# Seven block products in place of eight for the first expert layer of the last batch, with partial sums chained in PSUM

## The chip, the cores and the metric

The kernel runs on one core of one Trainium2 chip. The metric is the device time of one execution in microseconds (us). Before the change it was 373.66 us, the median of 3 runs (373.06 to 373.91). The profile comes from one execution of the kernel; its span, from the first to the last instruction, is about 1.8 us shorter than the device time of the same execution.

## The reference

Block-sorted attention is followed by a mixture of four experts. Only the second part is changed.

```python
def _moe_ref(x, domain_probs, w1, w2):
    N, D, E, F = (3072, 512, 4, 1024)     # from the setup
    p = domain_probs / (domain_probs.sum(-1, keepdims=True) + 1e-09)
    out = np.zeros((N, D), dtype=np.float32)
    for e in range(E):
        h = np.maximum(x @ w1[e], 0.0)          # first layer
        out += p[:, e:e + 1] * (h @ w2[e])      # second layer
    return out
```

`x` is the attention's output: 4 batches of 768 tokens. The kernel takes a batch's tokens in three chunks of 256. While it computes the experts of one batch, it interleaves the attention of the next one, so only the last batch has nothing beside it.

## The kernel before

The first layer (line L735 in the profile) multiplies 128x128 blocks of weights with 256 tokens at a time, 32 matmuls per expert and chunk. VectorE evicts the result: relu, times the expert's probability, into `Hb`. The second layer (L769) is already in seven block products. Its inputs are `Hb` and sums of its blocks (`Sb`), which VectorE makes in `h_sums`.

```python
def h_sums(e, which):                       # all on VectorE, two SBUF inputs each
    if which == 1:   tt(sm[0], blk(0, 1), blk(1, 1), ALU.add)
    elif which == 2: tt(sm[1], sm[0], blk(0, 0), ALU.subtract)
    elif which == 3: tt(sm[2], blk(0, 0), blk(0, 1), ALU.subtract)
    else:            tt(sm[3], blk(1, 0), sm[1], ALU.subtract)

def chunk_first(b, c, es, first, slot):
    for e in es:
        for g in range(2):
            ps = psm([P, 4, 2 * P], F32, ...)
            for f in range(4):
                for kc in range(NKC):                        # L735
                    nc.tensor.matmul(ps[:, f, :], w1sb[e][:, kc, ds((4 * g + f) * P, P)],
                                     xT[:, kc, ds(2 * c * P, 2 * P)],
                                     start=(kc == 0), stop=(kc == NKC - 1))
            nc.vector.scalar_tensor_tensor(out=Hb[:, e, ds(4 * g, 4), :], in0=ps[:], scalar=0.0,
                                           op0=ALU.max, in1=<probability>, op1=ALU.mult)
            if e > first:
                for w in ((1,), (2, 3))[g]:
                    h_sums(e - 1, w)                         # between the experts
            slot()                                           # work of the next batch's attention
```

The natural-order keys, values and queries of a batch come into tiles of a rotating pool, the queries into a single one:

```python
nat = ctx.enter_context(tc.tile_pool(name="nat", bufs=2))
...
natural[(b, "q")] = nat.tile([P, NPB, R, 2, D], F16, name=f"natq_{b}", tag="natq", bufs=1)
```

The loads of batch 1 are emitted early in the program, ahead of the first expert layer of batch 0 (`load_natural(1, ...)`, `load_queries(1, ...)`).

The softmax here doesn't subtract the row's maximum and nothing guards it: scores larger than these inputs give would overflow.

## Time and profile before

| | before |
|---|---|
| device time, median | 373.66 us |
| span of the profiled run | 371.0 us |
| TensorE busy | 362.8 us (98%) |
| last batch, chunk | 13.97 us first layer + 12.23 us second layer |
| the wait of TensorE for the queries of batch 1 | 1.8 us |

The prediction shows the page's first line, the chain of the last batch and the two stretches of its last chunk. Two more views matter here. The first is the page's list of groups: line, engine, operation, output and input, shapes, count; then the busy time and the mean nanoseconds of one; then the idle time of the engine before them, and what ended it.

```profile
L735 PE MATMUL ps_h<-xT,w 128*128 128x256 f16 x1440 | 163.3, 273 | 0.0
L741 DVE SCALAR_TENSOR_TENSOR Hb<-ps_h,pb 128x1024 f16<-128x1024 f32 x90 | 110.1, 1223 | 40.3 <-PE ps_h L735 38.7
```

The mean of 273 ns in the first line is the time of one matmul from issue to end. Matmuls overlap, so the cost of one in a row is the busy time over the count: 163.3/1440 = 0.113 us over the whole kernel, and 0.109 us in the last batch. VectorE's eviction of 1024 elements has 40.3 us of idle time ahead of it, nearly all of it waiting for TensorE: VectorE has time left.

The second view is the chain of work that ended last, where batch 1 starts (start, length, what):

```profile
68.92 6.63 DMA natq<-in_q_dram
...
75.56 7.31 DMA qT<-natq
```

Here transfers carry the chain for 14 us on end: the queries are loaded for 6.63 us, then transposed by a second transfer for 7.31 us, and TensorE waits for that at 82.9 us.

### The profile page before, as it was taken

The page shows a single profiled execution, that of the slowest core. Times are in us where ns is not written, and L with a number is a line of the kernel's source. Part 1 is how long each engine was busy: PE and PEld are TensorE (multiplying, and loading weights), DVE is VectorE, ACT ScalarE, POOL GpSimd, SP SyncE. Part 2 cuts the span into 40 slices and gives each one's busy share as a digit, 9 for nine tenths or more (in the row PEclk, how much of TensorE's full clock was granted, in tenths as well). Part 3 has the DMA queues.
Part 4 walks back from the last instruction along what each step waited for, and adds up shares of the span by engine and source line. Part 5 has one row for each costly group of instructions (what it writes and reads, how often), then busy time and mean ns, then how long its engine had stood idle before and what let it go on. Part 6 is the DMA issues. An engine that isn't in the chain of part 4 may idle for free.

```text
span 371.0 us, 9075 instructions
## 1 busy us (share of the span) xinstructions
PE 362.8 (98%) x3939; PEld 314.8 (85%) x3939; DVE 259.9 (70%) x469; ACT 87.8 (24%) x157; POOL 86.0 (23%) x122
## 2 busy tenths in 40 slices
PE   8899999989999999999999999999999999999996
PEld 8785858869888888998898888998888888888885
DVE  5654798666988784696695684696695693774873
ACT  2664330534230334222100335222101000000000
POOL 8872101803486303001911000000000001001001
PEclk9999999999999999999999999999999999999999
DMA  8999999998999868741972322604204101121001
GB/s 118 208 206 230 208 209 197 187 163 107 178 160 164 110 87 125 139 81 43 123 69 52 101 63 63 142 3 79 80 0 80 59 12 46 58 44 55 18 0 58
DMA packets 69748, 38.25 MB, mean 103 GB/s; under 512 B 40391, under 2 KB 64717, under 8 KB 69709
## 3 DMA queue, kind: packets, MB, share of 16 engines
q0 software_dynamic: 34640, 17.83, 39.1%
q1 hardware_dynamic: 35068, 19.85, 27.2%
q8 instruction: 31, 0.51, 0.5%
q14 instruction: 9, 0.07, 0.1%
HBM read 42.00 MB, written 6.34 MB: 130 GB/s over the span
## 4 chain that ended last, share of the span: by engine, by line
PE 85%; DMA 7%; DVE 4%; ACT 2%; POOL 1%; issue 1%; DVEq 0%; ACTq 0%
PE ps_h L735 39%; PE ps_p L769 33%; PE ps_h L640 3%; DMA xT<-xsl 3%; PE ps_o L675 3%; DMA qT<-natq 2%; DMA natq<-in_q_dram 2%; PE ps_s L398 1%; PE ps_a L430 1%; PE ps_k L379 1%; PE ps_v L346 1%; PE ps_mk L467 1%; DVE xsl L415 1%; PE ps_s L522 1%; DMA sn<-in_sort_net_dram 0%
## 5 line engine op out<-in xcount | busy, mean ns | idle before, releaser
L735 PE MATMUL ps_h<-xT,w 128*128 128x256 f16 x1440 | 163.3, 273 | 0.0
L735 PEld LDWEIGHTS <-w 128*128 128x128 f16 x1440 | 139.6, 98 | 17.3
L741 DVE SCALAR_TENSOR_TENSOR Hb<-ps_h,pb 128x1024 f16<-128x1024 f32 x90 | 110.1, 1223 | 40.3 <-PE ps_h L735 38.7
L769 PEld LDWEIGHTS <-Sb 128*128 128x128 f16 x720 | 69.8, 98 | 9.0 <-issue 0.3
L769 PEld LDWEIGHTS <-Hb 128*128 128x128 f16 x540 | 52.2, 98 | 6.1
L800 POOL TENSOR_TENSOR oa<-u,p 128x256 f32<-128x256 f32 x9 | 6.5, 721 | 175.7 <-issue 160.9
L769 PE MATMUL ps_p<-w,Sb 128*128 128x256 f16 x360 | 43.3, 273 | 0.1
L769 PE MATMUL ps_p<-w,Hb 128*128 128x256 f16 x360 | 43.1, 273 | 0.0
L769 PE MATMUL ps_p<-T,Sb 128*128 128x256 f16 x360 | 42.1, 273 | 0.0
L388 ACT CAST kT<-ps_k 64x384 f16<-64x384 f32 x48 | 22.7, 473 | 37.9 <-PE ps_k L379 37.0
L405 ACT ACTIVATE ET<-ps_s 96x768 f16<-96x768 f32 x24 | 18.0, 802 | 46.5 <-PE ps_s L398 46.5
L784 ACT COPY p<-ps_p 128x256 f32<-128x256 f32 x9 | 3.3, 372 | 90.5 <-PE ps_p L769 68.1
L114 POOL DMA_DIRECT2D natq<-in_q_dram x24 | 19.8, 851 | 13.3 <-DMA w<-in_moe_w_dram 9.3
L769 PE MATMUL ps_p<-T,Hb 128*128 128x256 f16 x180 | 21.6, 273 | 0.0
L720 DVE TENSOR_TENSOR Sb<-Sb,Hb 128x512 f16<-128x512 f16 x45 | 18.8, 418 | 0.4
L722 DVE TENSOR_TENSOR Sb<-Hb 128x512 f16<-128x512 f16 x45 | 18.8, 418 | 0.0
L718 DVE TENSOR_TENSOR Sb<-Hb 128x512 f16<-128x512 f16 x45 | 18.7, 416 | 0.0
L415 DVE TENSOR_TENSOR xsl<-ps_a,rz 96x512 f16<-96x512 f32 x24 | 16.5, 687 | 1.1 <-DMA xT<-xsl 0.3
L724 DVE TENSOR_TENSOR Sb<-Hb,Sb 128x512 f16<-128x512 f16 x45 | 16.6, 427 | 0.0
L798 DVE TENSOR_TENSOR u<-ps_p,p 128x256 f32<-128x256 f32 x9 | 3.8, 425 | 17.4 <-PE ps_p L769 17.4
L352 ACT CAST vo<-ps_v 128x768 f16<-128x768 f32 x12 | 9.5, 801 | 20.0 <-PE ps_v L346 19.3
L103 POOL DMA_DIRECT2D nat_k<-in_k_dram x8 | 6.1, 760 | 32.0 <-PE ps_k L379 27.1
(132 smaller groups left out, 298.3 us busy)
## 6 DMA issues: line engine op xcount, KB each, us to landing
w<-in_moe_w_dram POOLq DMA_DIRECT2D x7, 1024.0 KB, 26.5
pb<-p_dram SPq DMA_DIRECT2D x12, 512.0 KB, 5.1
nat_k<-in_k_dram POOLq DMA_DIRECT2D x8, 384.0 KB, 8.1
nat_v<-in_v_dram POOLq DMA_DIRECT2D x8, 384.0 KB, 8.7
vs<-vo SPq DMA_DIRECT2D x36, 66.0 KB, 4.5
natq<-in_q_dram POOLq DMA_DIRECT2D x24, 96.0 KB, 6.3
out_dram<-ob SPq DMA_DIRECT2D x9, 256.0 KB, 2.1
out_dram<-oa SPq DMA_DIRECT2D x8, 256.0 KB, 2.3
```

Of the source, the lines that this page charges most:

```text
L114: nc.gpsimd.dma_start(t[:, h // 2, :, h % 2, :], q[b, h].rearrange("(t p) d -> p t d", p=P))
L388: nc.scalar.copy(kT[ds(D * hh, D), r], pk[ds(D * r, D), hh].rearrange("p a (i c) -> p a i c", c=CP),)
L405: nc.scalar.activation(ETs[2 * (pr % 2) + hh][:, 0:S].rearrange("c (a x) -> c a x", a=2), pss[hh][0:BLK, :, 0:HS], AF.Exp, bias=0.0, scale ...
L415: nc.vector.tensor_tensor(xsl[:, :, hh, :].rearrange("c (a i) d -> c a i d", a=2), av[:, :, :, 0:D], rz[:].broadcast_to([BLK, 2, HB, D]), ...
L640: nc.tensor.matmul(ps[:, f % 2 if nq == 2 else f // 2, ds(0 if nq == 2 else (f % 2) * n, n)], w1sb[0][:, kc, ds((m * g + f) * P, P)], xT[: ...
L718: tt(sm[0], blk(0, 1), blk(1, 1), ALU.add)
L720: tt(sm[1], sm[0], blk(0, 0), ALU.subtract)
L722: tt(sm[2], blk(0, 0), blk(0, 1), ALU.subtract)
L724: tt(sm[3], blk(1, 0), sm[1], ALU.subtract)
L735: nc.tensor.matmul(ps[:, f, :], w1sb[e][:, kc, ds((4 * g + f) * P, P)], xT[:, kc, ds(2 * c * P, 2 * P)], start=(kc == 0), stop=(kc == NKC ...
L741: nc.vector.scalar_tensor_tensor(out=Hb[:, e, ds(4 * g, 4), :], in0=ps[:], scalar=0.0, op0=ALU.max, in1=pb[:, ds(e, 1), :].broadcast_to([P ...
L769: nc.tensor.matmul(ps[:], lhs(e, f), Ts[e][rhs][:, f, :], start=(e == es[0] and f == 0), stop=(e == E - 1 and f == KH - 1),)
```

## The change

The intent is to save an eighth of TensorE's multiplications in the first layer of the last batch: seven block products in place of eight, as the second layer does already. Each product is 8 matmuls of 128 columns. The partial sums that several products share are not added by VectorE: ScalarE copies product 1 from one PSUM bank into another, and the next products accumulate on top of it. The weight sums need space, which the attention's dead buffers give in the last batch; for that these buffers become slices of one large tile, the arena.

```diff
+    arena = const.tile([P, 4 * NW + NQ + 4 * 4 * P + R * 4 * VW], F16, name="arena")
 ...                                    # keys, values, queries, masks and vo become slices of it:
-            natural[(b, "q")] = nat.tile([P, NPB, R, 2, D], F16, name=f"natq_{b}", tag="natq", bufs=1)
+            natural[(b, "q")] = arena[:, ds(4 * NW, NQ)].rearrange("p (n t h d) -> p n t h d", n=NPB, t=R, h=2)
 ...                                    # attention tiles on 128 partitions in place of 96:
-            vs = att.tile([BLK, NB, 4, VW], F16, name=f"vs_{b}_{qd}", tag="vs")
+            vs = att.tile([P, NB, 4, VW], F16, name=f"vs_{b}_{qd}", tag="vs")[0:BLK]
 ...                                    # the loads of batch 1 are emitted later
+    def input_sums(e, n):              # 16 weight sums, in batch 2
+        nc.vector.tensor_tensor(a[dst], a[x], a[y], op)
+    def token_sums(c):                 # 4 sums of token blocks per chunk
+        ...
+    def last_banks(n):                 # re-divides the PSUM: banks X, Z, Q
+        ...
+        nc.tensor.matmul(last["X"][n][:], w1sb[0][:, 0, 0:P], w1sb[0][:, 1, 0:512], start=True, stop=True)
+    def seven(c, e):
+        def product(dst, lhs, rhs, first=False):
+            for f in range(KH):
+                for k in range(2):
+                    nc.tensor.matmul(
+                        dst[:, ds(f * P, P)], a[lhs][:, k, ds(f * P, P)], t[rhs][:, k, :],
+                        start=(first and f == 0 and k == 0), stop=(f == KH - 1 and k == 1), ...)
+        def p1(): product(Z, "a11", "b11", True);  nc.scalar.copy(X, Z)
+        def p5(): product(Q, "s1", "t1", True)
+        def p6(): product(X, "s2", "t2");          nc.scalar.copy(u2, X)
+        def p2(): product(Z, "a12", "b21");        finish(0, 0, Z)            # VectorE
+        def p7(): product(X, "s3", "t3");          nc.scalar.copy(u3, X); tt(t22, Q, u3, ALU.add)
+        def p4(): product(X, "a22", "t4");         finish(1, 0, X)            # VectorE
+        def p3(): product(Q, "s4", "b22");         tt(t12, Q, u2, ALU.add)
+        # blocks 22 and 12: relu on ScalarE, then the multiplication on GpSimd
+    def last_chunk(c):
+        ...                            # products of the four experts, then the second layer:
+        for e in range(E - 1):
+            h_sums(e, 1)
+        tt(oa1, product("p2", blk(1, 0), "b21"), p1[:], ALU.add)
+        ...
```

## The prediction

> **What bounds the kernel now.** I read the page's busy shares first, then its chain of work that ended last, then the busy time by stretch for the last batch, which is the only part whose arithmetic changes.
>
> ```profile
> PE 362.8 (98%) x3939; PEld 314.8 (85%) x3939; DVE 259.9 (70%) x469; ACT 87.8 (24%) x157; POOL 86.0 (23%) x122
> ...
> PE 85%; DMA 7%; DVE 4%; ACT 2%; POOL 1%; issue 1%; DVEq 0%; ACTq 0%
> ```
>
> ```profile
> 289.01 13.97 PE ps_h L735 x128
> 302.99 12.23 PE ps_p L769 x112
> ...
> 341.41 13.97 PE ps_h L735 x128
> 355.38 12.24 PE ps_p L769 x112
> ```
>
> The first fence is of the page, the second is the chain in order of time (start, length, what). TensorE is 98% busy and carries 85% of the chain; and from 289.01 on to 367.62 us the chain is TensorE alone: three chunks, each 128 matmuls of the first layer in 13.97 us and 112 of the second in 12.23 us, with no wait between them. The 3.4 us after 367.62 are the last sum and store and stay as they are. So one matmul of 256 columns costs 13.97/128 = 0.1091 us there, and what TensorE saves in a first layer is saved in full, unless a wait appears.
>
> ```profile
> core 0: us, PE busy (x) PEld busy (x) DVE busy (x) ACT busy (x) POOL busy (x), PEclk, DMA share, GB/s
> ...
> 341.40:355.40 14.00, 14.00 (x131) 12.55 (x129) 11.15 (x15) 0.00 (x0) 0.00 (x0) 1.00 0.10 39
> 355.40:367.60 12.20, 12.20 (x112) 10.69 (x110) 6.60 (x14) 1.12 (x3) 1.45 (x2) 1.00 0.04 12
> ```
>
> VectorE is busy 11.15 of 14.0 us in a first layer, ScalarE and GpSimd do nothing there. The change will use those two.
>
> The price of the new matmul (128 columns, each with a weight load of its own) is in the timeline: 30 of them in a row early on, and six in batch 1.
>
> ```profile
> 9.05 1.85 PE L241 MATMUL ps_w<-Hb 128*128 128x128 f16 x30
> ...
> 100.53 0.51 PE L379 MATMUL ps_k<-PIk,nat_k 128*128 128x128 f16 x6 [0.23 <-DVE xsl L415]
> 100.62 0.69 DVE L415 TENSOR_TENSOR xsl<-ps_a,rz 96x512 f16<-96x512 f32 x1
> 100.82 0.70 PEld L735 LDWEIGHTS <-w 128*128 128x128 f16 x7
> 100.87 0.82 PE L735 MATMUL ps_h<-xT,w 128*128 128x256 f16 x6
> ```
>
> One such matmul lasts 0.219 us by itself (that line's median). Thirty: (1.85-0.219)/29 = 0.0562 us each. Six different weights: (100.87-100.53)/6 = 0.057. I take 0.056.
>
> **What the Trainium skill says.** "TensorE: Matmul & The Clock Gate", section Back-to-back issue gap, gives N/2.4 + 2.5 ns for an isolated stream, 55.8 ns at 128 columns, but also a sustained 81 ns per pair of weight load and matmul at 128 columns. The trace agrees with the first (0.056) and not with the second, in short bursts only. "PSUM — Partial Sum Buffer", The four PSUM rules: a matmul without the first flag accumulates where an earlier matmul has set the bit, and ScalarE's writes leave these bits alone. That is what lets ScalarE copy product 1 into a second bank and the next products add on top; no run of before shows it. "SBUF — State Buffer", SBUF: two separate sides: a VectorE operation with two SBUF inputs and a GpSimd operation exclude each other for the whole instruction. The trace agrees:
>
> ```profile
> 366.46 0.72 POOL L803 TENSOR_TENSOR ob<-u,p 128x256 f32<-128x256 f32 x1 [1.03 <-DVE u L801]
> 366.48 0.99 DVE L804 TENSOR_TENSOR ob<-ob,u 128x256 f32<-128x256 f32 x1
> ```
>
> VectorE's sum takes 0.99 us beside GpSimd's, where the same size with one input in PSUM takes 0.425.
>
> **The change, part by part.**
>
> *TensorE, first layer.* Per chunk and expert, 32 matmuls of 256 columns become 7 products of 8 matmuls of 128 columns. Per chunk: 4 x 56 x 0.056 = 12.54 us in place of 13.97, so 1.43 saved; three chunks: 4.3 us. The columns fall by an eighth (8192 to 7168 per expert: 32 x 256 against 56 x 128), which alone would be 13.97/8 = 1.75; the fixed part of a matmul, paid 224 times in place of 128, takes the rest.
>
> *Added on TensorE:* two throw-away matmuls of 512 columns when the PSUM pools are re-divided, 0.2 us each: +0.4.
>
> *Weight sums.* Sixteen VectorE sums of 128x1024 f16, 0.69 us each as L706 has them, 11 us in all, plus four token sums of 128x256 (some 0.3 each, estimated) per chunk. They stand in batch 2. There VectorE waits in most second layers (busy 8.4 to 9 of 13 us), and the dead buffers' last readers are done well before by the order of instructions. The crowded place is the last chunk of batch 2: in 276.0 to 289.0 it is busy 8.4 us of 13.0, and gets nine of the sums (6 us) and four token sums. Walking its queue: oa's first half ended at 282.55 and gets three sums ahead of it, near 284; three more behind it, and the p6 sum ends near 287 in place of 286.0; one more, and the first token sum ends about 288.0, while TensorE, after p7 (287.1 plus 0.2), reaches the product that needs it at about 287.75. I put +0.3 for batch 2.
>
> *The pace of one expert.* Seven products of 0.446 us are 3.12 us. Sizes for 512 columns: ScalarE copies 256 in 0.372 (L784) and 384 in 0.473 (L388), so 512 in about 0.58; VectorE 0.69 (L415 has 0.687, half of L741's 1.22 plus the fixed part agrees); GpSimd has 0.72 for 256 in f32 (L803) and 1.04 for 512 in f16 (L319), so about 1.25 for 512 in f32 (estimate). Per expert ScalarE has five (2.9 us), VectorE four (2.8), GpSimd two (2.5): all three fit into 3.12, by little. A reader starts 0.24 us after TensorE has left a product (p1 of a second layer starts at 302.82, 16 x 0.109 later is 304.57, and its copy starts at 304.81). The tightest wait: product 1 ends at 0.45, its copy runs 0.69 to 1.27, product 2 may write that bank again at 1.31 and is due at 1.34, behind products 7 and 5. The second: product 7 ends 0.89, its copy ends 1.8, the VectorE sum 2.5, product 3 is due at 2.67. So it just fits. I charge 0.05 per expert for misfits: 12 x 0.05 = +0.6.
>
> *The turn into the second layer.* All Hb sums, formerly between the experts, now come after the last expert, and two of the four Hb blocks come from GpSimd. Times from the start of the last expert's product 7, TensorE without waits: p2 of the second layer ends at 4.84, p4 at 6.58, and p5 then needs the bank of p2, freed by VectorE's p2 sum; p5's last quarter, at 7.89, needs the last expert's first Hb sum. GpSimd still has four multiplications of 1.25: 0.5 to 1.8, 1.9 to 3.1, 3.1 to 4.4, and the last not before 4.7, because its input (product 3 at 3.1, VectorE to 4.0, ScalarE to 4.6) is late. VectorE reaches its Hb sums, two SBUF inputs each, at 4.0 and must wait for GpSimd. If it gets in at 4.4, three sums of 0.34 and the p2 sum end at 5.9, in time; GpSimd's last then runs 5.5 to 6.75, the next three sums wait for it and end at 7.8, and the last expert's first sum at 8.2 makes p5 wait 0.3. If GpSimd keeps the port through its fourth, to 6.0, the p2 sum ends at 7.4 and p5 waits 0.85. I take 0.5 per chunk, +1.5.
>
> Sum: -4.3 + 0.4 + 0.3 + 0.6 + 1.5 = -1.5 us, rounded to 372.0 from 373.66.
>
> Batches 0 to 2 keep their order on every engine apart from the sums; loads of batch 1 are emitted later but stand at the same place of the queue. I give them 0.
>
> **The rivals.**
> 1. *Nothing waits.* The queues fit as counted and GpSimd is quicker than I think: -4.3 + 0.4 + 0 to 0.3 = 369.9. For it: every wait in the expert loop has a slack of 0 or more, so the order was fitted to these durations. Against: slack of 0.03 us.
> 2. *An engine takes over.* If a ScalarE copy from PSUM into PSUM, which before nowhere has, is 0.1 longer, product 2 waits each time and the five copies reach 3.4 us, so the pace is ScalarE's: 12 x 0.3 = 3.6 us back, near 374.5 with the turn's wait.
> 3. *The short matmuls run at the skill's sustained 81 ns.* 672 x 0.081 = 54.4 against 41.9 us: +12.5, near 386. Against it, besides the 0.056: L430's 16 matmuls of 65 columns with a weight load each take 0.48 us, 0.030 each, so a load does not cost 0.08.
> 4. *The lock at the turn is worse*, 1.2 us per chunk: 374.
>
> **Range and chances.** 369.6 is rival 1 with a little luck, 374.4 is rivals 2 or 4; I hold 8 in 10 between. Faster by 2% would need 7.5 us, more than TensorE saves in all: 1%. Slower by 2% needs rival 3 or a mistake of mine: 3%.
>
> **What would show it.** Right: first layers of the last batch near 12.6 to 12.9 us with 224 matmuls at 0.056; a wait of TensorE of about half a microsecond at the second layer's p5, released by VectorE, with GpSimd busy until then; second layers near 12.7 net of the next chunk's products. Wrong: a pace of one expert well over 3.2 us with ScalarE without idle time (rival 2); matmul pitch of 0.08 (rival 3); no wait at p5 (rival 1); or a loss in batch 2 over 1 us, at the weight sums.

## The result, and the profile after

The changed kernel ran in 369.52 us, median of 4 runs (369.09 to 370.15), beside 373.79 us of the kernel before on the same chip (373.06 to 374.86). A ratio in this document is the mean time of one kernel's runs over that of the other's runs of the same rounds, so it is not quite the ratio of the medians quoted. Here it is 0.9885, with a 95% interval of 0.9857 to 0.9913. The prediction had 372.0 and the range 369.6 to 374.4, so the result lies just below the range.

The page's first line and the chain by engine:

```profile
PE 358.5 (97%) x4229; PEld 313.8 (85%) x4229; DVE 277.5 (75%) x521; ACT 121.5 (33%) x217; POOL 118.6 (32%) x146
...
PE 80%; DMA 11%; DVE 5%; POOL 1%; issue 1%; ACT 1%; DVEq 0%; ACTq 0%
```

TensorE has 4.3 us less work in more instructions, ScalarE and GpSimd have 38% more each, and VectorE 18 us more. The chain is still TensorE's.

The chain in the last batch, one expert of the new first layer (start, length, what):

```profile
293.60 0.45 PE ps_Q L981 x8
294.04 0.45 PE ps_Z L981 x8
294.49 0.45 PE ps_X L981 x8
294.94 0.45 PE ps_Q L981 x8
295.38 0.45 PE ps_Z L981 x8
295.83 0.89 PE ps_X L981 x16
296.72 0.45 PE ps_Q L981 x8
```

Seven products of 8 matmuls follow on each other without a gap, and the same point of the next expert comes at 296.72: 3.12 us per expert, 56 matmuls, 0.0557 us each. No other engine appears. The groups that run beside them:

```profile
L994 POOL TENSOR_TENSOR Hb<-tmp,pb 128x512 f16<-128x512 f32 x24 | 30.9, 1293 | 20.2 <-ACT tmp L993 19.0 <-DVE Sb L725 0.6
L993 ACT ACTIVATE tmp<-tmp 128x512 f32<-128x512 f32 x24 | 15.2, 635 | 3.2 <-DVE tmp L1025 2.6 <-DVE tmp L1017 0.6
L1016 ACT COPY tmp<-ps_X 128x512 f32<-128x512 f32 x12 | 7.1, 591 | 0.6 <-PE ps_X L981 0.6
L1001 ACT COPY ps_X<-ps_Z 128x512 f32<-128x512 f32 x12 | 6.8, 570 | 15.9 <-PE ps_Z L981 15.9
```

The copy from PSUM into PSUM takes 0.570 us, the copies out of it 0.586 (L1008) and 0.591, and each of the two relus 0.635. The five durations of ScalarE add up to 0.570 + 0.586 + 0.591 + 2 x 0.635 = 3.02 of the 3.12 us, but this sum is not what ScalarE needs. The timeline of one expert, with the TensorE product (p2) that must wait for the first copy:

```profile
294.57 0.57 ACT L1001 COPY ps_X<-ps_Z 128x512 f32<-128x512 f32 x1 [0.21 <-PE ps_Z L981]
295.05 0.59 ACT L1016 COPY tmp<-ps_X 128x512 f32<-128x512 f32 x1
295.22 0.61 PE L981 MATMUL ps_Z<-xT,w 128*128 128x128 f16 x8
296.37 0.59 ACT L1008 COPY tmp<-ps_X 128x512 f32<-128x512 f32 x1 [0.20 <-PE ps_X L981]
```

Operations that follow directly on each other overlap: the second copy starts 0.48 us after the first, which lasts 0.57. ScalarE is idle for 0.21 and 0.20 us in an expert in the middle of the loop, waiting for TensorE, so it has about 0.4 us to spare. p2 starts 0.08 us after the copy that it waits for has ended.

At the turn into the second layer the chain leaves TensorE, once in each chunk. The timeline of that stretch, without the rows that matter less (start, length, engine, line, operation, count, idle time before it and what ended it), and under it what the trace says of the three sums in it (shortest, median and longest in ns):

```profile
302.10 2.51 POOL L994 TENSOR_TENSOR Hb<-tmp,pb 128x512 f16<-128x512 f32 x2
...
304.14 2.49 DVE L725 TENSOR_TENSOR Sb<-Hb 128x512 f16<-128x512 f16 x3
...
304.97 1.38 POOL L994 TENSOR_TENSOR Hb<-tmp,pb 128x512 f16<-128x512 f32 x1 [0.36 <-ACT tmp L993]
305.01 1.91 PE L1069 MATMUL ps_Q<-T,Hb 128*128 128x256 f16 x16
...
306.56 0.41 DVE L1090 TENSOR_TENSOR oa<-ps_Q,p 128x256 f32<-128x256 f32 x1
...
307.02 1.95 PE L1069 MATMUL ps_Q<-w,Sb 128*128 128x256 f16 x16
```

```profile
L725 DVE TENSOR_TENSOR Sb<-Hb x3: 412/747/1487, 304.1 to 305.1; 128x512 f16<-128x512 f16 x3
```

TensorE issues p4 from 305.01 on; 16 matmuls at 0.109 us end at 306.76, and p5 starts only at 307.02. It needs the bank that VectorE's sum at 306.56 reads. That sum had its input since about 305.2, but VectorE was still in the third of its three `Hb` sums, which began at 305.14 and took 1.487 us in place of 0.412: GpSimd's multiplication ran from 304.97 to 306.35. The chunks follow at 25.09 us (p5 at 307.02, 332.11 and 357.20) where they took 26.20 before.

The stretch where batch 1 starts, in the chain:

```profile
69.16 5.88 DMA arena<-in_q_dram
...
75.06 7.09 DMA qT<-arena
```

Both transfers are a little shorter than before (5.88 for 6.63, 7.09 for 7.31), and TensorE waits 0.8 us for them, not 1.8.

To split the gain I cut the chain of each kernel where the second layer of batch 2's last chunk begins, and where the last product ends:

| | up to the cut | from the cut to TensorE's end | then |
|---|---|---|---|
| before | 276.30 | 91.32 | 3.4 |
| after | 275.93 | 88.47 | 3.3 |
| difference | -0.4 | -2.85 | -0.1 |

The second column is firm: two more runs of the changed kernel give 88.47 too, and a second one of the kernel before 91.33. The first column varies by 0.4 to 0.7 us between profiles of one kernel, so it needs several. Over all kept profiles whose clock was not lowered before the cut, it is 276.30 and 276.91 us with the old buffers (before, before_again) and 274.72 to 276.33, mean 275.69, in thirteen with the new place of the query buffer: some 0.9 us less. The second column shows that the last batch alone gave 2.85 us, where the prediction had 1.5.

### The profile page after: what moved, and what is told of

Its sections match the earlier page's. It is cut to its first block, busy times and chain, and to the rows that moved or that the text cites. A ratio compares the mean times of both kernels' runs of the same rounds, so it can differ in the third digit from the quotient of the medians.

```text
span 367.7 us, 9859 instructions
## 1 busy us (share of the span) xinstructions
PE 358.5 (97%) x4229; PEld 313.8 (85%) x4229; DVE 277.5 (75%) x521; ACT 121.5 (33%) x217; POOL 118.6 (32%) x146
## 4 chain that ended last, share of the span: by engine, by line
PE 80%; DMA 11%; DVE 5%; POOL 1%; issue 1%; ACT 1%; DVEq 0%; ACTq 0%
PE ps_h L742 28%; PE ps_p L777 23%; PE ps_Q L1069 8%; PE ps_X L981 4%; DMA w<-in_moe_w_dram 4%; DMA xT<-xsl 3%; PE ps_Q L981 3%; PE ps_Z L981 3%; PE ps_o L682 3%; DMA qT<-arena 2%; DMA arena<-in_q_dram 2%; PE ps_h L647 1%; PE ps_s L405 1%; DVE Sb L725 1%; PE ps_a L437 1%
## 5 line engine op out<-in xcount | busy, mean ns | idle before, releaser
L742 PE MATMUL ps_h<-xT,w 128*128 128x256 f16 x1056 | 121.0, 273 | 0.0
L742 PEld LDWEIGHTS <-w 128*128 128x128 f16 x1056 | 102.1, 98 | 13.1
L748 DVE SCALAR_TENSOR_TENSOR Hb<-ps_h,pb 128x1024 f16<-128x1024 f32 x66 | 80.7, 1223 | 29.5 <-PE ps_h L742 29.0
L777 PEld LDWEIGHTS <-Hb 128*128 128x128 f16 x396 | 38.1, 98 | 4.6
L994 POOL TENSOR_TENSOR Hb<-tmp,pb 128x512 f16<-128x512 f32 x24 | 30.9, 1293 | 20.2 <-ACT tmp L993 19.0
L777 PE MATMUL ps_p<-w,Hb 128*128 128x256 f16 x264 | 31.6, 273 | 0.0
L777 PE MATMUL ps_p<-w,Sb 128*128 128x256 f16 x248 | 29.9, 273 | 0.1
L120 POOL DMA_DIRECT2D arena<-in_q_dram x24 | 19.9, 853 | 12.1 <-DMA w<-in_moe_w_dram 9.7
L981 PEld LDWEIGHTS <-w 128*128 128x128 f16 x384 | 23.3, 98 | 0.4
L981 PEld LDWEIGHTS <-arena 128*128 128x128 f16 x288 | 17.4, 98 | 0.1
L993 ACT ACTIVATE tmp<-tmp 128x512 f32<-128x512 f32 x24 | 15.2, 635 | 3.2 <-DVE tmp L1025 2.6
```

The lines of the kernel that those rows point to most:

```text
L120: nc.gpsimd.dma_start(t[:, h // 2, :, h % 2, :], q[b, h].rearrange("(t p) d -> p t d", p=P))
L777: nc.tensor.matmul(ps[:], lhs(e, f), Ts[e][rhs][:, f, :], start=(e == es[0] and f == 0), stop=(e == E - 1 and f == KH - 1),)
L981: nc.tensor.matmul(dst[:, ds(f * P, P)], a[lhs][:, k, ds(f * P, P)], t[rhs][:, k, :], start=(first and f == 0 and k == 0), stop=(f == KH - ...
L994: nc.gpsimd.tensor_tensor(Hb[:, e, ds(i * KH, KH), ds(j * P, P)], src.rearrange("p (f x) -> p f x", f=KH), pb[:, ds(e, 1), ds(j * P, P)].b ...
```

## The experiments

Sixteen runs followed. My theory after the result had four parts: the first layer is 1.47 us faster per chunk and nothing else waits in it; the turn costs about 0.3 us per chunk, through VectorE's order behind GpSimd; the weight sums cost nothing; and the new buffer layout gives about 1 us at the start of batch 1. The rivals were that these shares are chance, that the later emission of the loads is what helps, and that ScalarE is near the bound.

### after_again: the changed kernel unedited, five rounds

> The changed kernel once more, unedited, in five rounds, to learn how large the gain is: the two profiles differ by 3.3 us of span, the medians of four runs by 4.3. Theory A (the gain lies in the last batch alone): 3.1 us, from counting TensorE between the start of the second layer of batch 2's last chunk and the end (91.48 before, 88.40 after). Theory B (about 1 us more is gained in batches 0 to 2, where I had put 0): 4.0 to 4.5 us.

Measured: 369.8 us (median) beside 373.96, ratio 0.989 (0.9864 to 0.9917). The gain of 4 us stands.

### layout_only: arena, wider tiles and later loads, but the old last batch

```diff
-        if b == B - 1:                    # of the changed kernel
-            for c in range(R // 2):
-                last_chunk(c)
-            break
-                if b == B - 2: ...        # weight sums, prepare_last, token_sums, last_begin
```

> The changed kernel with its one arena, the later emission of batch 1's loads and the wider tiles, but with the old last batch, no weight sums, no re-divided PSUM. Theory A: 0 against the kernel before, within 0.3 us. Theory B: 0.7 to 1.3 us faster than the kernel before. In the profile the last batch must run at 13.97 and 12.23 us per layer as before.

Measured: 372.81 us beside 373.96, ratio 0.9976 (0.9949 to 1.0002). The interval touches 1, but the trace agrees with a gain: TensorE waits 1.3 us for the queries and is busy 54.64 us from 62 to 118 us, where the kernel before has 1.8 and 53.85.

### layout_and_sums: the same, with the sixteen weight sums in batch 2

```diff
+                if b == B - 2:
+                    for cc, n, e, m in PLAN_A:
+                        if (cc, n) == (c, at[0]):
+                            input_sums(e, m)
```

The result of the sums isn't used; the one that would overwrite a weight writes a dead block instead.

> As layout_only, with the sixteen VectorE weight sums of 128x1024 added in batch 2 at the places of the change (the fourth of each expert writes a dead block in place of the weights, so the result stays right; nothing reads them). My prediction's step: +0.3 us over layout_only (with four token sums too, which are left out here). The trace of the changed kernel says 0: its second layer of batch 2's last chunk took 14.26 us, which is the old 12.71 plus 1.34 for the three products moved in and 0.21 for one throw-away matmul. So 0 within 0.2 us against layout_only; if the sums cost anything, batch 2's chunks are longer by it.

Measured: 372.5 us beside 373.96, ratio 0.9968 (0.9943 to 0.9992), no more than layout_only. The stretch of batch 2's last chunk from 276 to 289 us, first of layout_only, then of layout_and_sums (length, then the busy time of TensorE, its weight loads, VectorE, ScalarE and GpSimd with their instructions):

```profile
276.00:289.00 13.00, 13.00 (x133) 11.69 (x132) 8.30 (x19) 1.12 (x3) 1.44 (x2) 1.00 0.33 57
```

```profile
276.00:289.00 13.00, 13.00 (x133) 11.70 (x131) 12.29 (x26) 1.12 (x3) 1.77 (x2) 1.00 0.32 57
```

VectorE takes 4 us more in there and reaches 12.29 of 13.0, and TensorE still does the same 133 matmuls without a gap. The sums cost nothing, even in the crowded place. The four token sums are not in this run; in the changed kernel, which has them, the chain too stays on TensorE without a gap through this stretch.

### extra_scalar: one ScalarE copy per expert twice

```diff
             product(X, "s2", "t2")
             nc.scalar.copy(u2, X)
+            nc.scalar.copy(u2, X)
```

> The changed kernel with one copy of ScalarE repeated for each expert (product 6 to u2, written twice, same values): 0.59 us more of ScalarE in each of twelve experts. If the expert loop has room, nothing changes. If it just fits, as I counted (five operations of 0.57 to 0.64 make 3.02 of 3.12 us), ScalarE now needs 3.6 us and sets the pace: each pair of experts in the loop takes about 3.6 in place of 3.13, nine times, so about 4 us slower than the changed kernel, about level with the kernel before.

Measured: 372.53 us beside 373.96, ratio 0.9954 (0.9927 to 0.9982), so 2.7 us over after_again. In the chain one product of an expert now takes 0.61 us in place of 0.45, and the same product of the next expert comes 3.42 us later:

```profile
293.28 0.61 PE ps_X L981 x8
...
296.70 0.61 PE ps_X L981 x8
```

The copy adds 0.59 us to ScalarE and only 0.30 us to this pace: the rest goes into the idle time, which falls from about 0.4 us to 0.16 in each expert. From the cut to TensorE's end the kernel takes 91.73 us in place of 88.47, so 3.3 us more where I expected 4. I had added ScalarE's durations without their overlap, and so had counted its room too small. The pace without the extra copy is TensorE's. The run doesn't show that ScalarE then becomes the bound, as it still has idle time: the trace's longest waits of TensorE (1.4 us in three) are for the repeated copy, which holds the bank that the next product needs. Rival 2 of the prediction had the right place, but it needs more than the room that was there.

### turn_order: VectorE's sums at the turn in another order

```diff
-        for e in range(E - 1):
-            h_sums(e, 1)
+        h_sums(0, 1)
         tt(oa1, product("p2", blk(1, 0), "b21"), p1[:], ALU.add)
+        for e in range(1, E):
+            h_sums(e, 1)
 ...
-        for w in range(1, 4):
+        for w in range(2, 4):
             h_sums(E - 1, w)
```

Nothing is added or left out.

> The changed kernel with VectorE's queue reordered at the turn into each second layer, no operation added: one Hb sum, then the p2 sum that frees the bank of p5, then the other three first Hb sums. If the wait at p5 (0.26 to 0.36 us, plus 0.04 inside p5) comes from VectorE's sums standing behind GpSimd's multiplications and in front of the p2 sum, it goes: three times about 0.35, so 1.0 us faster than the changed kernel, with p5 starting right behind p4. If it comes from elsewhere (the last GpSimd block itself), it stays or moves into p5's last quarter: 0.

Measured: 368.35 us beside 374.45, ratio 0.9843 (0.9808 to 0.9879). The timeline of the same turn:

```profile
303.68 0.74 DVE L725 TENSOR_TENSOR Sb<-Hb 128x512 f16<-128x512 f16 x1
...
304.50 1.27 POOL L994 TENSOR_TENSOR Hb<-tmp,pb 128x512 f16<-128x512 f32 x1 [0.36 <-ACT tmp L993]
304.54 1.91 PE L1069 MATMUL ps_Q<-T,Hb 128*128 128x256 f16 x16
304.81 0.42 DVE L1089 TENSOR_TENSOR oa<-ps_Q,p 128x256 f32<-128x256 f32 x1 [0.40 <-PE ps_Q L1069]
305.16 1.56 DVE L725 TENSOR_TENSOR Sb<-Hb 128x512 f16<-128x512 f16 x3
...
306.29 1.91 PE L1069 MATMUL ps_Q<-w,Sb 128*128 128x256 f16 x16
```

The sum of p2, which has one input in PSUM, runs beside GpSimd's multiplication in its ordinary 0.42 us. The `Hb` sums after it wait for GpSimd, and nobody waits for them. p5 starts at 306.29, which is p4's 304.54 plus 16 x 0.109: no wait. In the chain the second layer is one unbroken run of 80 matmuls there, from 302.96 on, and no TensorE wait is left in the whole last batch. From the cut to TensorE's end it takes 87.45 us in this run and in its repeat, against 88.47: the turn cost 1.02 us, 0.34 per chunk. The run is no direct comparison of times with the changed kernel; turn_again is.

### turn_vector: the last block of the last expert finished on VectorE

```diff
-        now[12]()                         # relu on ScalarE, multiplication on GpSimd
+        now["12v"]()                      # finish(0, 1, t12): both at once on VectorE
```

> The changed kernel with the last expert's second GpSimd block (the one of product 3) finished on VectorE in one operation, so that neither GpSimd's 1.3 us nor ScalarE's 0.63 us stands there: GpSimd is done at 304.6 in the first chunk's times in place of 306.35. Same theory: the wait at p5 goes, three times about 0.3, so 0.9 us faster than the changed kernel. VectorE gains 0.69 us of work per chunk, which it has room for. If the wait has another cause: 0, or slower by up to 0.6.

Measured: 368.68 us beside 374.45, ratio 0.9854 (0.9818 to 0.989), no wait at the turn either, and again 87.45 us from the cut to TensorE's end. Taking GpSimd out of the turn has the same effect as reordering VectorE around it. Two different edits remove the same wait, so GpSimd's last multiplication beside VectorE's sums was its cause.

### no_dummy: without the two matmuls of 512 columns (a wrong result)

```diff
-        nc.tensor.matmul(last["X"][n][:], w1sb[0][:, 0, 0:P], w1sb[0][:, 1, 0:512], start=True, stop=True)
```

> The changed kernel without its two throw-away matmuls of 512 columns at the re-division of PSUM. TensorE shows each as 0.21 us between its neighbours, so 0.4 us faster than the changed kernel; 0 if their time only stands in for a wait on the banks, which the next matmul would then have.

Measured: 369.27 us beside 374.45, ratio 0.9865 (0.9827 to 0.9904), and a wrong result, with a relative error of 0.0903. I had not expected that. In the prediction I had called these matmuls throw-away; they aren't. The X banks get their first data from ScalarE's copy, and products 6, 7 and 4 add to it with no start flag of their own. The likely explanation is the rule of the hidden bits that the prediction cites from the Trainium skill ("PSUM — Partial Sum Buffer", The four PSUM rules): a matmul without the first flag adds only where an earlier matmul has set the bit, and ScalarE's writes don't set it. By that rule the two matmuls set it once for all 512 columns of each X bank; without them the bits would be what the former use left, and some products would overwrite instead of adding. This is argued: no run looks at the bits themselves. The run's profile had a granted clock of 0.99, lowered in the first 36 us, so I draw nothing from its total. The last batch was at full clock, and from the cut to TensorE's end it takes 88.05 us, 0.42 less than the changed kernel: the two matmuls cost what they last.

### best_order: turn_order without the two matmuls (a wrong result)

The edit is those of turn_order and no_dummy together.

> Both at once, the reordered turn and no throw-away matmuls: 1.4 us faster than the changed kernel, near 368.2 us, some 5.5 us (1.5%) faster than the kernel before. TensorE between the start of the second layer of batch 2's last chunk and the end should then take 88.40 - 1.4 = 87.0 us.

Measured: 368.58 us beside 374.45, ratio 0.9847 (0.9809 to 0.9884), and the same error of 0.0903, so it is no candidate. From the cut to TensorE's end it takes 87.02 us; 87.0 was expected.

### before_again: the kernel before against itself

> The kernel before against itself, as a control of the method: ratio 1.000, with an interval that shows what a difference of 1 us is worth here; and a second profile of it. Theory B (the new layout shortens batch 1's start): its profile again shows about 2 us of idle TensorE between 62 and 118 us, as the first did (53.85 of 56.0 busy), where the kernels with the arena have 54.0 to 54.9. Theory A (chance): some other value, 54.0 to 55.

Measured: 373.71 us beside 373.74, ratio 1.0005 (0.9989 to 1.0021). TensorE is busy 53.50 us from 62 to 118 us, near the 53.85 of the first trace and a microsecond under the kernels with the new layout.

### moved_loads: the kernel before with only the loads of batch 1 emitted later

```diff
-    for qd in range(2):                   # ahead of batch 0's first expert layer
-        for nm in ("v", "k"):
-            load_natural(1, nm, qd)
-        if qd == 0:
-            load_queries(1, range(2))
 ...                                       # and the same five lines after second_layer0(0, ...)
```

> The kernel before with only the loads of batch 1 emitted later, where the change has them; buffers, last batch and sums as before. GpSimd's order is the same as before. If the later emission alone makes the 1 us that the layout gained: 0.7 to 1.3 us faster than before, and 54.5 or more of 56 us of TensorE busy between 62 and 118 us. If it is the arena or chance: 0.

Measured: 373.93 us beside 373.74, ratio 1.0016 (0.9993 to 1.004). The later emission alone gives no gain that these runs can see.

### after_third and turn_again: the changed kernel and turn_order side by side

> The changed kernel once more, on the same chip as the next run, to compare the two directly: ratio to before about 0.989, as in the two looks so far.

> The changed kernel with the reordered VectorE queue at the turn once more: 1.0 us (0.27%) under after_third, ratio to before about 0.986. In the trace TensorE goes from p4 to p5 without a wait in all three chunks.

Measured on one chip, beside 373.74 us of the kernel before: after_third 370.14 us, ratio 0.9929 (0.989 to 0.9968), with one run of 374.61 that pulls the mean up; turn_again 368.65 us, ratio 0.9874 (0.9853 to 0.9896). The medians differ by 1.5 us; the profiled stretch from the cut to TensorE's end again by 1.02 (88.47 and 87.45). The means, without that one run, differ by 1.0 (369.89 and 368.91), as expected. turn_order is faster than both kernels, and its result is right; by the measure of 2% it too counts as the same.

### layout_again: layout_only once more, with three kernels on which part of the layout it is

> The same kernel as layout_only, to halve its interval. If the layout is worth about 1 us at the start of batch 1, the ratio is 0.996 to 0.999 again (about 1 us under the kernel before) and TensorE is busy 54.5 to 54.9 us in the stretch from 62 to 118 us; if layout_only's 1.1 us was chance, the ratio is 0.999 to 1.001 and the busy time 53.5 to 53.9 us.

Measured: 372.48 us beside 374.24, ratio 0.9957 (0.9927 to 0.9987). Now the interval excludes 1. TensorE is busy 54.75 us from 62 to 118 us.

### arena_narrow: layout_only with the attention tiles on 96 partitions again

```diff
-            vs = att.tile([P, NB, 4, VW], F16, ...)[0:BLK]
+            vs = att.tile([BLK, NB, 4, VW], F16, ...)      # and two more tiles likewise
```

> Layout_only with the attention tiles (sorted values, sorted block outputs) on 96 partitions again, so the one large buffer alone is left of the layout. If the large buffer is the cause: TensorE busy 54.5 to 54.9 us from 62 to 118 us and a ratio of 0.996 to 0.999. If the wider tiles are the cause (they change which buffer follows which): 53.5 to 53.9 us and a ratio near 1.

Measured: 372.75 us beside 374.24, ratio 0.9961 (0.9934 to 0.9987), busy 54.80 us. The tiles narrowed here have no part in it (the `ET` tiles stay wide).

### fixed_queries: the kernel before with the query buffer in a place of its own

```diff
+    natq_fixed = const.tile([P, NPB, R, 2, D], F16, name="natq_fixed")
-            natural[(b, "q")] = nat.tile([P, NPB, R, 2, D], F16, name=f"natq_{b}", tag="natq", bufs=1)
+            natural[(b, "q")] = natq_fixed
```

> The kernel before with only the query buffer in a fixed place. If it was the release of the query buffer as a whole that held the query loads of batch 1 back: busy 54.5 us or more from 62 to 118 us, the transposes of the queries done by 82.5 us, and a ratio of 0.996 to 0.999. If the cause is where the other buffers lie: no change, busy 53.5 to 53.9 us and a ratio of 0.999 to 1.001.

Measured: 373.46 us beside 374.24, ratio 0.9971 (0.9938 to 1.0005). Inconclusive: the interval touches 1, and the profiled run had a granted clock of 0.986, with two slices of 0.7 near the start, so that TensorE came late and waited for nothing at batch 1. Its busy time is no evidence. (Taking only runs with a granted clock of 0.998 or more, 4 of 6 here and 7 of 11 of the kernel before, it is 0.7 us faster, which settles nothing either.)

### fixed_and_moved: both, the query buffer's own place and the later loads

The edit is those of fixed_queries and moved_loads together.

> The kernel before with the query buffer in a fixed place and batch 1's loads emitted later, as the changed kernel has them. If the two together are the cause, busy 54.5 us or more from 62 to 118 us and a ratio of 0.996 to 0.999; if the place of the key, value and mask buffers is needed too, 53.5 to 53.9 us and a ratio near 1.

Measured: 372.41 us beside 374.24, ratio 0.9963 (0.9932 to 0.9994), as good as the whole layout. The busy time from 62 to 118 us (the columns are those of the stretches above), first the kernel before, then fixed_and_moved:

```profile
62.00:118.00 56.00, 53.85 (x589) 46.76 (x587) 43.88 (x81) 18.49 (x33) 26.83 (x33) 1.00 1.56 162
```

```profile
62.00:118.00 56.00, 54.79 (x597) 47.60 (x595) 44.82 (x82) 18.86 (x34) 27.36 (x33) 1.00 1.39 164
```

TensorE does 0.94 us more work in the same stretch. What it waits for in there, in total, times and longest, first in moved_loads, then in fixed_and_moved:

```profile
PE ps_s L398 <- DMA qT<-natq: 2.2, 1, 2.2
```

```profile
PE ps_s L399 <- DMA qT<-natq_fixed: 1.0, 1, 1.0
```

The two kernels differ in the edit to the query buffer alone, and the wait for the query transposes falls from 2.2 to 1.0 us. But that edit does more than move one buffer: the new tile stands second in its pool, so what is allocated after it moves too. Both programs show `Hb`, the weights and the key and value buffers 6144 bytes further on in each partition, and other waits before the query loads of batches 2 and 3 (none other for batch 1). Which of these shifts helps is not separated. A second caution: in moved_loads's profile the granted clock fell to 0.69 from 85 to 90 us, after this wait; whether a longer wait brings on such a dip was not tested. The loads don't start earlier (the first pair at 68.09 us in moved_loads and 68.51 in fixed_and_moved); the transfers end sooner (transposes of 6.59 us for 7.45 on the chain). From the issue of the first load to the end of the transposes it is 14.76, 15.51 and 15.22 us in before, before_again and moved_loads, and 13.78 to 14.20 in twelve profiles with the new place; a thirteenth, turn_vector, has 14.69 and so no such gain. Why the transfers are faster is open.

## Why the prediction was wrong

The sign was right and the size was not: 1.5 us predicted, about 4.2 measured (369.8 for 373.96). Term by term, in the order of the prediction's sum:

| step of the prediction | predicted | measured | from |
|---|---|---|---|
| TensorE, first layer | -4.3 | -4.4 | 3 x (13.97 - 224 x 0.0558) |
| two matmuls of 512 columns | +0.4 | +0.43 | 0.22 and 0.21 in the chain |
| weight sums, batch 2 | +0.3 | 0 | layout_and_sums |
| misfits in the pace of an expert | +0.6 | about 0 | 3.12 us per expert, no wait |
| the turn | +1.5 | +1.02 | turn_order |
| batches 0 to 2 | 0 | -0.8 to -1.3 | layout runs, cut |
| sum | -1.5 | about -3.8 to -4.3 | |

The first five measured terms add up to -2.95, and the cut in the chain gives -2.85 for the last batch, so 0.1 us at most is left for anything unseen.

**The step that failed** in kind is "I give them 0" for batches 0 to 2. It carries about two fifths of the error; the rest are the three charges below, which were too large. I had compared the order of instructions and found it unchanged, and took that for unchanged time. But I had not looked at what the stretch of batch 1 waits for. The chain showed it in the profile before: 14 us of query load and transpose, with TensorE idle at its end. A change that moves the buffers of exactly these transfers deserved a range of its own. The size of this term: five runs with a new place for the query buffer and the old arithmetic (layout_only, layout_and_sums, layout_again, arena_narrow, fixed_and_moved) have ratios from 0.9957 to 0.9976, mean 0.9965, so 1.3 us. Some of this is the clock: the kernel before had it under 0.998 in 4 of 11 runs. With such runs left out on both sides the five are 0.8 to 1.3 us faster, mean 1.1. Their busy time from 62 to 118 us is 0.8 to 1.0 us over that of the first trace, and a little more over the control's. Kernels without it (before_again, moved_loads) have 1.0005 and 1.0016. That the edit to the query buffer is enough together with the later loads is shown by fixed_and_moved beside moved_loads. Whether it is enough by itself is not settled, nor which of the buffers that it moves matters, and the mechanism inside the transfers is open.

**The three charges.** These steps were right in kind and too large. "I charge 0.05 per expert for misfits": the durations fit in each of the twelve experts. The slack that I had put at 0.03 us for product 2 was 0.08, and ScalarE's operations overlapped, which my sum of 2.9 us had left out; the 12 charges were 0.6 us of nothing. "I put +0.3 for batch 2": the same; VectorE was filled to 12.29 of 13.0 us and nobody waited. "I take 0.5 per chunk" for the turn: it was 0.34. Here I had drawn two cases and taken the mean of them. The trace shows something between: GpSimd had the port through its fourth multiplication, as in the second case, but VectorE had got two of its three sums in before that, so the sum of p2 ended at 6.8 us by the prediction's clock, where I had 5.9 and 7.4. The wait, who caused it and whom it hit were as told.

**Rivals.** Rival 1 ("nothing waits", 369.9) came closest by its number, for the wrong reason: the turn did wait. Rival 2 (ScalarE) was refuted by the pace of 3.12 us and the copy's 0.570; extra_scalar shows what it would have cost. Its "near 374.5" was also summed too low: with its own 3.6 and the turn's 1.5 it comes to 374.9. Rival 3 (81 ns per matmul) fell: 0.0557 us per matmul over whole experts. Rival 4, 1.2 us per chunk at the turn, was more than three times too much.

**What I had misread without a cost** is the pair of "throw-away matmuls". Their time was right, but their purpose wasn't: no_dummy shows that the result depends on them.

## What to carry to other kernels

When a change moves buffers, price the stretches that wait for transfers in these buffers, even if the order of instructions stays; a control with the new layout and the old arithmetic separates the two. Here a loop whose durations fitted with a small positive slack cost nothing in any of its rounds, so a charge is better kept for the places where the chain can leave the bounding engine. Where VectorE and GpSimd must overlap, put the VectorE operation that TensorE waits for ahead of those with two SBUF inputs: that alone was worth 1.0 us here.

## What the Trainium skill lacked or had wrong

- "TensorE: Matmul & The Clock Gate", section Back-to-back issue gap, gives a sustained 81 ns per pair of weight load and matmul at 128 columns, and about 56 ns for an isolated stream. With a weight load for each matmul, 672 matmuls in the last batch kept to 0.0558 us, expert after expert; the isolated figure was the sustained one here.
- "SBUF — State Buffer", section SBUF: two separate sides, has the lock between VectorE and GpSimd right. The runs add its price at a turn: a sum of 0.412 us took 1.487 us beside one GpSimd multiplication, while a VectorE sum with one input in PSUM ran beside it in 0.42 us, its ordinary time.
- "PSUM — Partial Sum Buffer", The four PSUM rules, tells the rule of the bits, and that products add to what ScalarE wrote where a matmul had written before. It advises a start value of 0 and only mentions a dummy matmul; the case here, with a start value that isn't 0, is not worked through. With one matmul with the first flag over the whole bank beforehand the result was right; leaving it out gave an error of 0.0903.
- No page that I read says that the place of buffers in SBUF can change the time of a load and a transposing transfer. With the query buffer in another place, and what is allocated after it shifted, the wait for them was 1.0 in place of 2.2 us; the cause is open.
